# Squared-ReLU attention and two feed-forward networks on one core: another order where the last attention chunk meets the networks

## The chip, the cores and the metric

The kernel runs on one core of a Trainium2 chip. The metric is the device time of one execution in microseconds; the lower the better. Engines are named as in the profile: PE (matrix products; PEld loads their weights), DVE and ACT (element-wise work), POOL, and SP, which issues the transfers.

## The reference

```python
scores = (1.0 / S) * np.matmul(z, z.transpose(0, 2, 1))   # B=2, S=3008, d_qk=64
x = u * np.matmul(np.maximum(scores, 0.0) ** 2, v)        # d_model=256; then x: 6016 x 256
h = x @ w_in                                              # 256 -> 2048
y = (h - np.tanh(h)) @ w_out                              # 2048 -> 256
gate = 1.0 / (1.0 + np.exp(-(y @ w_gate)))                # 256 -> 1536
out = (gate * (y @ w_val)) @ w2_out                       # 1536 -> 256
```

The weights come as float64, everything else as float32.

## The kernel before, in words

The 6016 tokens are cut into 12 chunks of up to 512 (six to a batch; the last of each batch has 448). Every float32 operand of a product is split into a high and a low part, and a product is three passes: high by high, low weights by high, high weights by low.

The work is a list of **units** (`units`, L460 to L466). An attention unit is one chunk of queries against two tiles of 128 keys; there are 12 to a chunk (KP). The first 11 chunks are `HalfAttention`: its PE products use 64 rows of the array each, two at a time. The last chunk (11) is plain `Attention`, whose products use all 128 rows; its scores are four products over stacked high and low parts. A unit of the first network, `Ffn1`, takes 256 of the 2048 hidden columns (N1 = 8 units a chunk), one of the second, `Ffn2`, takes 128 of 1536 (N2 = 12). In this text A0 to A11 are the units of the last attention chunk, F*c*.*f* is unit f of `Ffn1` on chunk c, and G*c*.*f* one of `Ffn2`.

A unit has a `front` (its first PE products, into one of two PSUM buffers: `s`, `h` or `gv`), a `mid1` and `mid2` on ACT and DVE, and a `back` (PE products that add into `acc`). The loop at L562 takes a step per unit n: the small jobs noted in `todo` for n, the front of n, mid1 of n, mid2 of n-1, a pending `end`, and the backs of older units (`ahead`: two units on for attention, three for the networks). `end` runs one unit after the last back of a chunk; for `Ffn1` it copies `acc` into `yh` on ACT and writes `yl` on DVE, the two parts of y that every `Ffn2` front of the chunk reads. Each engine takes its instructions in the order in which this loop writes them.

The order of the units at the end of attention is set by sort keys (L462 to L466): A*i* has i; F0.f has START + f; F*c*.f for later chunks 12 + 12(c-1) + 1.5 f; G*c*.f has 12 + 12 c + f + LAG. Weights are split into high and low by `todo` jobs: two per `Ffn1` unit just ahead of it, and those of `Ffn2` from L535 on, W2_LAG units after F0.0.

Of the kernel before, what the change touches and what calls it, by code (L numbers as in the profile page):

```python
# [30 lines left out]
def squared_relu_attention__then__two_ffns(  # L31
# [24 lines left out]
    KP = KT // 2  # L56
# [3 lines left out]
    assert HALF * 2 == P and ND == 2 and DQ * 2 == P and KT % 4 == 0  # L60
    WARM, FILL = 6, 2
    LATE = 1
    START = 2.5
    LAG = 5
    W2_LAG = 16

    ring = ctx.enter_context(tc.tile_pool(name="ring", bufs=42))
    work = ctx.enter_context(tc.tile_pool(name="work", bufs=9))
# [19 lines left out]
    NC = len(chunks)  # L88
# [164 lines left out]
    class Attention(Unit):  # L253
# [5 lines left out]
            self.first, self.last = i == 0, i == KP - 1  # L259

        def front(self):
            b, n = self.b, self.n
            self.ps = psf.tile([P, 2, NQ], F32, tag="f", name="s")
            for e in range(2):
                i = 2 * self.i + e
                k = z_t[b, i // 4][:, 0, (i % 4) * P : (i % 4 + 1) * P]
                for h in range(2):
                    nc.tensor.matmul(self.ps[:, e, :n], k, z_t[b, self.j][:, h, :n], start=h == 0, stop=h == 1)  # L268
# [190 lines left out]
    N1, N2 = FF1 // P // 2, FF2 // P  # L459
    units = [HalfAttention(c, i) for c in range(NC - 1) for i in range(KP)]  # L460
    n_att = len(units)
    mixed = [(i, 0, Attention(NC - 1, i)) for i in range(KP)]  # L462
    mixed += [(START + f, 1, Ffn1(0, f)) for f in range(N1)]
    mixed += [(KP + (c - 1) * N2 + f * N2 / N1, 1, Ffn1(c, f)) for c in range(1, NC) for f in range(N1)]
    mixed += [(KP + c * N2 + f + LAG, 2, Ffn2(c, f)) for c in range(NC) for f in range(N2)]
    units += [t[2] for t in sorted(mixed, key=lambda t: t[:2])]  # L466
    start, where = {}, {}
    for n, u in enumerate(units):
# [6 lines left out]
    def at(n, fn):  # L475
        todo.setdefault(max(n, 0), []).append(fn)


    for b in range(B):
# [21 lines left out]
        for j in range(NZ):  # L501
            n = need[j] + early[j]
# [7 lines left out]
    for c in range(NC):  # L510
        at(start[0, c] + 2, lambda c=c: load_u(c))
        n = start[1, c]
# [7 lines left out]
    n = 8  # L520
    half = start[0, NZ]
    split = {}
    for k, p in enumerate(parts):
# [5 lines left out]
        if half - 14 < n < half + 4:  # L529
            n = half + 4  # L530
    for f in range(N1):
        n = where[1, 0, f]
        at(n - 3, split["wi1_", f // 2][f % 2])
        at(n - 2, split["wo1_", f // 2][f % 2])
    for f in range(N2 // 2):  # L535
        n = where[1, 0, 0] + W2_LAG + 2 * f
        assert n < where[2, 0, 2 * f]
        for i, key in enumerate(("wg2_", "wv2_", "wo2_")):
            at(min(n + i, where[2, 0, 2 * f] - (i < 2)), split[key, f // 2][f % 2])

    warm = const.tile([P, 1], F32, name="warm")
    square_max = const.tile([P, 1], F32, name="square_max")
# [86 lines left out]
```

## Time and profile before

| what | us |
|---|---|
| median of 3 executions (lowest, highest) | 1589.08 (1588.97, 1589.38) |
| the profiled execution | 1588.82 |
| its span, first to last instruction | 1587.0 |
| PE busy | 1578.1 |
| DVE busy | 1106.9 |
| ACT busy | 1039.8 |

The profile page shows for each engine how much of the span it is busy. A timeline row gives the start in us from the span's start, the time until the last of its instructions is done, the engine, line, operation, tile written and tiles read, shapes and count; in brackets stands idle time before it and who ended it. The time from one PE row's start to the next is what a row costs, since products overlap at their ends. The page's clock row stands at 9 (90% or more of full speed) in every slice, and the mean granted clock is 0.999.

### The profile page before, as it was taken

The numbers are of one execution on the slowest core, as the hardware profiler recorded it, in microseconds if no ns is written. First come the engines' busy times: TensorE is split into PE (matmuls) and PEld (weight loads), VectorE is DVE, ScalarE is ACT, GpSimd is POOL, SyncE is SP. The second block draws the span as 40 slices with busy tenths as digits, with TensorE's granted clock in tenths as the row PEclk, the third lists the DMA queues.
The fourth block names the chain that finished last, engine by engine and source line by source line (L and its number), as shares of the span: only waits on it lengthen the run. The fifth ranks groups of instructions, "written<-read, shape, count | busy, mean of one in ns | idle before, by whom it ended". The sixth has DMA issues, their size and how long they took to land.

```text
span 1587.0 us, 21490 instructions
## 1 busy us (share of the span) xinstructions
PE 1578.1 (99%) x8988; PEld 1339.8 (84%) x8988; DVE 1106.9 (70%) x1254; ACT 1039.8 (66%) x1249; POOL 0.2 (0%) x4
## 2 busy tenths in 40 slices
PE   9999999999999999999999999999999999999998
PEld 7888889888888788888888888888888888888888
DVE  8988898988788986566566656576656566655542
ACT  8667778666679976566665666666566665656532
POOL 0000000000000000000000000000000000000000
PEclk9999999999999999999999999999999999999999
DMA  6222232221100000000000000000000000000000
GB/s 226 81 81 80 86 114 79 81 81 54 39 27 1 23 3 0 27 1 15 12 1 25 1 27 1 27 0 1 25 0 27 0 27 1 0 26 1 14 1 25
DMA packets 28178, 53.28 MB, mean 34 GB/s; under 512 B 1969, under 2 KB 10161, under 8 KB 28081
## 3 DMA queue, kind: packets, MB, share of 16 engines
q1 hardware_dynamic: 28080, 51.91, 9.7%
q8 instruction: 70, 1.15, 0.3%
q14 instruction: 28, 0.22, 0.0%
HBM read 39.58 MB, written 12.32 MB: 33 GB/s over the span
## 4 chain that ended last, share of the span: by engine, by line
PE 96%; DVE 2%; issue 1%; ACT 1%; DMA 0%; DVEq 0%; SPq 0%
PE acc L234 30%; PE gv L246 24%; PE acc L346 20%; PE h L246 16%; PE s L313 5%; PE s L268 1%; DMA raw_wg<-w_gate 0%; DVE ah L329 0%; DVE e L80 0%; DVE z L80 0%; ACT a L327 0%; ACT a L324 0%; PE acc L559 0%; DVE th L393 0%; DVE al L80 0%
## 5 line engine op out<-in xcount | busy, mean ns | idle before, releaser
L80 DVE TENSOR_TENSOR e<-h,th 128x1024 f32<-128x1024 f32 (+1 forms) x96 | 115.4, 1202 | 285.0 <-ACT sq L388 285.0
L346 PE MATMUL acc<-ah,v 64*128 64x512 f32 (+1 forms) x2068 | 297.2, 385 | 0.7 <-DVE sum L360 0.7
L346 PEld LDWEIGHTS acc<-ah,v 64*128 64x128 f32 x2068 | 215.4, 184 | 30.9 <-DVE sum L360 1.3
L387 ACT ACTIVATE th<-h 128x1024 f32<-128x1024 f32 (+1 forms) x96 | 97.0, 1010 | 216.2 <-PE h L246 216.2
L246 PE MATMUL h<-xh,wi 128*128 128x512 f32 (+1 forms) x768 | 233.8, 386 | 0.8 <-DVE e L80 0.8
L234 PE MATMUL acc<-p,wo 128*128 128x512 f32 (+1 forms) x864 | 215.5, 385 | 0.0
L234 PE MATMUL acc<-gh,wo 128*128 128x512 f32 (+1 forms) x768 | 204.7, 386 | 0.5 <-DVE yl L80 0.4
L324 ACT ACTIVATE a<-s 128x1024 f32<-128x1024 f32 (+2 forms) x133 | 134.3, 1010 | 90.3 <-PE s L313 88.5
L234 PEld LDWEIGHTS acc<-p,wo 128*128 128x128 f32 x864 | 162.2, 188 | 30.0
L437 ACT ACTIVATE sg<-gv 128x512 f32<-128x512 f32 (+1 forms) x144 | 84.6, 588 | 156.7 <-PE gv L246 156.7
L346 PE MATMUL acc<-al,v 64*128 64x512 f32 (+1 forms) x1034 | 180.9, 386 | 0.1
L80 DVE TENSOR_TENSOR al<-a,ah 128x1024 fp32r<-128x1024 f32 (+3 forms) x146 | 173.6, 1189 | 7.6 <-DVE ah L329 0.5
L246 PE MATMUL gv<-yh,wg 128*128 128x512 f32 (+1 forms) x576 | 175.3, 385 | 0.0
L246 PE MATMUL gv<-yh,wv 128*128 128x512 f32 (+1 forms) x576 | 175.0, 385 | 0.0
L438 DVE TENSOR_TENSOR sg<-gv,sg 128x512 f32<-128x512 f32 (+1 forms) x144 | 98.3, 683 | 106.5 <-ACT sg L437 106.4
L246 PEld LDWEIGHTS h<-xh,wi 128*128 128x128 f32 x768 | 144.1, 188 | 28.3 <-DVE e L80 1.3
L234 PEld LDWEIGHTS acc<-gh,wo 128*128 128x128 f32 x768 | 144.1, 188 | 28.1 <-DVE yl L80 1.2
L246 PE MATMUL h<-xl,wi 128*128 128x512 f32 (+1 forms) x384 | 147.9, 385 | 0.0
L327 ACT ACTIVATE a<-a 128x1024 f32<-128x1024 f32 (+2 forms) x133 | 139.1, 1047 | 4.2
L393 DVE COPY_PREDICATED th<-m,e 128x1024 f32<-128x1024 uint32 (+1 forms) x96 | 131.7, 1371 | 10.2 <-ACT wv L194 0.5
L346 PEld LDWEIGHTS acc<-al,v 64*128 64x128 f32 x1034 | 111.3, 184 | 16.9 <-DVE al L80 2.8
L246 PEld LDWEIGHTS gv<-yh,wv 128*128 128x128 f32 x576 | 108.1, 188 | 20.2
(100 smaller groups left out, 2263.7 us busy)
## 6 DMA issues: line engine op xcount, KB each, us to landing
raw_wo<-w_out SPq DMA_DIRECT2D x14, 512.0 KB, 5.8
u<-uT SPq DMA_DIRECT2D x10, 512.0 KB, 7.3
x<-u SPq DMA_DIRECT2D x10, 512.0 KB, 3.1
xl<-x SPq DMA_DIRECT2D x10, 512.0 KB, 3.7
outT<-o SPq DMA_DIRECT2D x20, 256.0 KB, 2.1
vraw<-v SPq DMA_DIRECT2D x9, 512.0 KB, 6.5
raw_wi<-w_in SPq DMA_DIRECT2D x8, 512.0 KB, 8.6
zraw<-zT SPq DMA_DIRECT2D x12, 256.0 KB, 5.9
```

The lines of the kernel that those rows point to most:

```text
L80: nc.vector.tensor_tensor(out=out, in0=a, in1=b, op=ALU.subtract)
L234: nc.tensor.matmul(acc[d][:, :n], wt[:, wi, w, d * P : (d + 1) * P], hl[ai], start=first and m == 0, stop=last and m == len(passes) - 1,)
L246: nc.tensor.matmul(ps, w[:, wi, d, fi * P : (fi + 1) * P], xs[xi][:, d, :n], start=m == 0, stop=m == len(passes) - 1)
L268: nc.tensor.matmul(self.ps[:, e, :n], k, z_t[b, self.j][:, h, :n], start=h == 0, stop=h == 1)
L313: nc.tensor.matmul(self.ps[:, e, :n], z_t[b, i // 4][r, ki ^ x, c : c + P], q[r, qi ^ x, :n], start=m == 0, stop=m == 2)
L324: nc.scalar.activation(a[:, t, :n], self.ps[:, t, :n], AF.Relu, scale=SCALE)
L327: nc.scalar.activation(s, s, AF.Square)
L346: nc.tensor.matmul(acc[h][d][:, :n], vt[r, w, e, d * P : (d + 1) * P], self.hl[a][r, e, :n], start=self.first and banks[k] not in banks[:k ...
L387: nc.scalar.activation(t, h, AF.Tanh)
L393: nc.vector.copy_predicated(t, m.bitcast(U32), e)
L437: nc.scalar.activation(s[:, :n], self.ps[:, 0, :n], AF.Sigmoid)
L438: nc.vector.tensor_tensor(out=s[:, :n], in0=self.ps[:, 1, :n], in1=s[:, :n], op=ALU.mult)
```

## The change

Four edits.

- The first two units of the last attention chunk (A0, A1) make their scores with `HalfAttention.front`: six products of 64 rows in place of four of 128.
- START goes from 2.5 to 1.5: F0.0 comes after A1 and not after A2, and all of chunk 0's `Ffn1` a unit sooner.
- The units of G0 get keys 12 + 1 + f·16/12 in place of 12 + 5 + f: the first follows F1.0, and the twelve are spread over 16 key steps.
- The weights of `Ffn2` are split three units ahead of the G0 unit that first reads them; W2_LAG is gone.

```diff
-    START = 2.5
+    START = 1.5
     LAG = 5
-    W2_LAG = 16
+    LAG0 = 1
...
         def front(self):
+            if self.i < 2:
+
+                HalfAttention.front(self)
+                return
             b, n = self.b, self.n
...
-    mixed += [(KP + c * N2 + f + LAG, 2, Ffn2(c, f)) for c in range(NC) for f in range(N2)]
+    mixed += [(KP + LAG0 + f * (N2 + LAG - LAG0) / N2, 2, Ffn2(0, f)) for f in range(N2)]
+    mixed += [(KP + c * N2 + f + LAG, 2, Ffn2(c, f)) for c in range(1, NC) for f in range(N2)]
...
     for f in range(N2 // 2):
-        n = where[1, 0, 0] + W2_LAG + 2 * f
-        assert n < where[2, 0, 2 * f]
+        n = where[2, 0, 2 * f] - 3
         for i, key in enumerate(("wg2_", "wv2_", "wo2_")):
-            at(min(n + i, where[2, 0, 2 * f] - (i < 2)), split[key, f // 2][f % 2])
+            at(n + i, split[key, f // 2][f % 2])
```

What it does to the order shows best at three places. The names are those of the tiles; a number behind a name tells one buffer from another.

**DVE where y of chunk 0 is made.** `e`, `th`, `th` are the mid1 of an `Ffn1` unit, `gl` its mid2, `yl` the end of chunk 0. Before, the unit whose mid1 stands here is F1.1:

```order
L80 TENSOR_TENSOR e_6343<-h_6327,th_6341 128x1024
L392 TENSOR_TENSOR th_6341<-th_6341,sq_6340 128x1024
L393 COPY_PREDICATED th_6341<-m_6342,e_6343 128x1024
L80 TENSOR_TENSOR gl_6352<-th_6287,gh_6351 128x1024
L80 TENSOR_TENSOR yl0_6356<-acc0_5810,yh0_6355 128x512
L80 TENSOR_TENSOR yl0_6356<-acc1_5811,yh0_6355 128x512
```

Now it is F1.0, and behind `yl` stands at once `sg` of G0.0, which is made from y:

```order
L80 TENSOR_TENSOR e_6308<-h_6292,th_6306 128x1024
L396 TENSOR_TENSOR th_6306<-th_6306,sq_6305 128x1024
L397 COPY_PREDICATED th_6306<-m_6307,e_6308 128x1024
L80 TENSOR_TENSOR yl0_6317<-acc0_5790,yh0_6316 128x512
L80 TENSOR_TENSOR yl0_6317<-acc1_5791,yh0_6316 128x512
L442 TENSOR_TENSOR sg_6347<-gv_6334,sg_6347 128x512
```

On PE, between the front of F1.0 (`h_6292`) and the front of G0.0 (`gv_6334`) stands only the back of A10, 12 products, of which the last two and the next rows are:

```order
L234 MATMUL acc0_5699<-al_6244,v1_10_3459 128x448
L234 MATMUL acc1_5700<-al_6244,v1_10_3459 128x448
L246 MATMUL gv_6334<-yh0_6316,wg2_0_6232 128x512 x2
L246 MATMUL gv_6334<-yl0_6317,wg2_0_6232 128x512
L246 MATMUL gv_6334<-yh0_6316,wg2_0_6232 128x512 x2
```

The reader of y has moved up to one unit behind the end that writes it; before, three `Ffn1` fronts and backs lay between.

**DVE around the last unit of chunk 0's first network (F0.7).** Before, the split of chunk 1's x (`xl1`) stands ahead of F0.7's chain:

```order
L80 TENSOR_TENSOR xl1_6003<-xl1_6003,xh1_6185 128x1024
L80 TENSOR_TENSOR e_6204<-h_6188,th_6202 128x1024
L392 TENSOR_TENSOR th_6202<-th_6202,sq_6201 128x1024
L393 COPY_PREDICATED th_6202<-m_6203,e_6204 128x1024
L279 CAST ah_6220<-a_6217 128x2x448
```

Now it stands inside it, ahead of `gl`, which the back of F0.7 reads:

```order
L80 TENSOR_TENSOR e_6181<-h_6165,th_6179 128x1024
L396 TENSOR_TENSOR th_6179<-th_6179,sq_6178 128x1024
L397 COPY_PREDICATED th_6179<-m_6180,e_6181 128x1024
L80 TENSOR_TENSOR xl1_6026<-xl1_6026,xh1_6189 128x1024
L283 CAST ah_6200<-a_6197 128x2x448
L80 TENSOR_TENSOR al_6201<-a_6197,ah_6200 128x2x448
L80 TENSOR_TENSOR gl_6205<-th_6179,gh_6204 128x1024
```

ACT has the same move: `xh1` now stands between F0.7's four functions and A9's. On PE the back of F0.7 has come nearer too: after the front of F0.7 stand four score products of A9, the back of F0.6, the back of A8, eight score products (A10, A11), and then it. Before, the front of F1.0 lay between as well.

**DVE where y of chunk 1 is made.** Before, the two `yl` stand behind a unit of `Ffn2` and ahead of the next `Ffn1` chain:

```order
L438 TENSOR_TENSOR sg_6919<-gv_6906,sg_6919 128x512
L80 TENSOR_TENSOR p_6922<-sg_6887,p_6922 128x512
L80 TENSOR_TENSOR yl1_6926<-acc0_6439,yh1_6925 128x512
L80 TENSOR_TENSOR yl1_6926<-acc1_6440,yh1_6925 128x512
L80 TENSOR_TENSOR e_6953<-h_6937,th_6951 128x1024
```

Now they stand behind the chain of F2.1:

```order
L80 TENSOR_TENSOR e_6976<-h_6960,th_6974 128x1024
L396 TENSOR_TENSOR th_6974<-th_6974,sq_6973 128x1024
L397 COPY_PREDICATED th_6974<-m_6975,e_6976 128x1024
L80 TENSOR_TENSOR p_6984<-sg_6938,p_6984 128x512
L80 TENSOR_TENSOR yl1_6988<-acc0_6420,yh1_6987 128x512
L80 TENSOR_TENSOR yl1_6988<-acc1_6421,yh1_6987 128x512
```

The first back of chunk 2 (F2.0) writes into the PSUM buffers that these two read, so it waits for them. On PE, between the front of F2.1 and that back stand now the back of a G unit (6 products) and the front of another (12).

## Rows read from the trace of the kernel before

**Rows 1.** The page, part 1: PE busy, share of the span.

```profile
PE 1578.1 (99%) x8988; PEld 1339.8 (84%) x8988; DVE 1106.9 (70%) x1254; ACT 1039.8 (66%) x1249; POOL 0.2 (0%) x4
```

**Rows 2.** Waits of PE from 430 to 600 us: total, times, longest.

```profile
PE h L246 <- DVE e L80: 0.8, 1, 0.8
PE acc L234 <- DVE yl L80: 0.4, 1, 0.4
```

**Rows 3.** Stretches: length, busy time (instructions) of each engine, clock, DMA, GB/s.

```profile
444.65:448.61 3.96, 3.96 (x30) 2.84 (x28) 3.89 (x6) 3.36 (x5) 0.00 (x0) 1.00 0.00 0
...
541.02:543.74 2.72, 2.72 (x13) 2.06 (x11) 2.64 (x3) 2.72 (x5) 0.00 (x0) 1.00 0.00 0
543.74:547.50 3.76, 3.29 (x14) 2.36 (x14) 3.66 (x5) 3.70 (x5) 0.00 (x0) 1.00 0.00 0
...
552.94:556.80 3.86, 3.02 (x14) 2.37 (x14) 3.62 (x4) 3.72 (x5) 0.00 (x0) 1.00 0.71 240
556.80:559.84 3.04, 3.01 (x13) 2.17 (x12) 3.04 (x4) 3.00 (x5) 0.00 (x0) 1.00 0.00 0
```

**Rows 4.** Timeline of PE, where the pieces spoken of begin.

```profile
1.48 2.93 PE L559 MATMUL acc<-blank 128*128 128x512 f32 x6 [1.48 <-DVE blank L548]
...
449.63 0.73 PE L346 MATMUL acc<-ah,v 64*128 64x512 f32 x4
...
468.22 0.63 PE L234 MATMUL acc<-gl,wo 128*128 128x512 f32 x2
...
518.84 0.97 PE L268 MATMUL s<-z 128*128 128x448 f32 x4
...
528.38 1.07 PE L234 MATMUL acc<-gh,wo 128*128 128x512 f32 x4
...
536.27 0.97 PE L234 MATMUL acc<-ah,v 128*128 128x448 f32 x4
...
544.27 1.56 PE L234 MATMUL acc<-gh,wo 128*128 128x512 f32 x4 [0.38 <-DVE yl L80]
```

**Rows 5.** Timeline of DVE around F0.0.

```profile
458.49 1.22 DVE L364 TENSOR_TENSOR u<-sum,u 128x1024 f32<-128x1024 f32 x1
...
466.57 1.22 DVE L80 TENSOR_TENSOR gl<-th,gh 128x1024 fp32r<-128x1024 f32 x1
```

**Rows 6.** Timeline of ACT around F0.7.

```profile
517.40 1.04 ACT L220 CAST xh<-xl 128x1024 fp32r<-128x1024 f32 x1
519.04 1.03 ACT L387 ACTIVATE th<-h 128x1024 f32<-128x1024 f32 x1 [0.60 <-PE h L246]
...
523.17 0.90 ACT L274 ACTIVATE a<-s 128x896 f32<-128x896 f32 x1
...
525.17 1.05 ACT L400 CAST gh<-th 128x1024 fp32r<-128x1024 f32 x1
```

**Rows 7.** Timeline of DVE around F0.7.

```profile
519.24 1.22 DVE L80 TENSOR_TENSOR xl<-xl,xh 128x1024 fp32r<-128x1024 f32 x1
...
523.67 1.41 DVE L393 COPY_PREDICATED th<-m,e 128x1024 f32<-128x1024 uint32 x1
525.09 0.63 DVE L279 CAST ah<-a 128x896 fp32r<-128x896 f32 x1
...
526.83 1.22 DVE L80 TENSOR_TENSOR gl<-th,gh 128x1024 fp32r<-128x1024 f32 x1
```

**Rows 8.** Timeline of DVE where y of chunk 0 is made.

```profile
541.10 1.42 DVE L393 COPY_PREDICATED th<-m,e 128x1024 f32<-128x1024 uint32 x1
542.40 1.22 DVE L80 TENSOR_TENSOR gl<-th,gh 128x1024 fp32r<-128x1024 f32 x1
543.53 1.29 DVE L80 TENSOR_TENSOR yl<-acc,yh 128x512 fp32r<-128x512 f32 x2
```

**Rows 9.** Timeline of DVE where y of chunk 1 is made.

```profile
708.16 0.68 DVE L80 TENSOR_TENSOR p<-sg,p 128x512 fp32r<-128x512 f32 x1
708.76 1.28 DVE L80 TENSOR_TENSOR yl<-acc,yh 128x512 fp32r<-128x512 f32 x2
712.98 1.23 DVE L80 TENSOR_TENSOR e<-h,th 128x1024 f32<-128x1024 f32 x1 [2.94 <-ACT sq L388]
```

## The prediction

> **What bounds the kernel now.** I read the page first: PE is busy 99% of the span [rows 1], so only PE time counts, and a change pays only by fewer or cheaper products or by waits that PE no longer has. Then PE's own waits: between 430 and 600 us, where the change works, the list has two, 0.8 and 0.4 us [rows 2]. That list shows only time in which PE stands quite still. To see what a wait costs with all that follows, I cut PE's timeline into pieces of 12 full products. An undisturbed piece takes 2.72 us, so 0.227 a product; three pieces take 3.76, 3.86 and 3.04 [rows 3]. They lie where four fronts of the first network stand close together, F1.0 to F1.3, and ACT and DVE are full (3.7 of 3.8 us). The excess is 1.04 + 1.14 + 0.32 = 2.5 us. That is all that spreading G0 can win. Last I read the timelines of ACT and DVE around the four places where the change alters who stands ahead of whom, and asked there: when is the operand ready, and when does PE now come for it?
>
> **Scores of A0 and A1.** The stretch from A0's scores to A1's holds 4 score products and 24 products of 64 rows in pairs, and takes 3.96 us [rows 3]. In 64 rows the scores are three pairs of 448 columns, 3 × 0.227 × 448/512 = 0.60, and the 12 pairs behind them 12 × 0.227 = 2.72: 3.32 together, 0.64 less. A1's scores start at 448.61 and the next products at 449.63 [rows 4], 1.02 now, 0.60 then: 0.42 less. The change from 64 to 128 rows then comes once, at F0.0's front, as it came at A2's scores. The gain is 1.06, at least 0.4 (the products saved alone, 2 × 0.2) and at most 1.2.
>
> **G0 sooner and stretched.** `Ffn1` and `Ffn2` units now alternate, F1.0, G0.0, F1.1, G0.1 and so on; the three slow pieces go: -2.5 us, surely within -1.5 and -2.6.
>
> **Wait 1, F0.0's `gl`.** With START a unit lower, the product `u` of chunk 10 (`end`, L364) is written behind F0.0's mid1 and not ahead of it, so on DVE it stands between F0.0's predicated copy and its `gl`. `u` takes 1.13 us until the next can start (of its 1.22) [rows 5]. `gl` was done at 466.57 + 1.22 = 467.79, PE came for it at 468.22 [rows 4, 5]: 0.43 to spare. The pieces of PE between front and back of F0.0 are the same 40 products in another order. So 1.13 - 0.43 = **0.70** of new wait, between 0.3 and 0.9.
>
> **Wait 2, F0.7's back.** Let T be the end of F0.7's front, 518.84 [rows 4]. PE came to F0.7's back at 528.38, T + 9.54. Now there stand between 12 score products and 12 of A8's back, 448 columns each, and 12 of F0.6's back: 2 × 2.4 + 2.7 = 7.5 to 7.6. On ACT, A9's functions began at T + 4.33 and `gh` two us later [rows 6]; with `xh` in front (about 0.95) `gh` starts at T + 7.28 and is done at T + 8.33: 0.75 of wait. Then 4 products (0.91) to about T + 9.3. On DVE the predicated copy starts at T + 4.83 and holds DVE 1.30 us (to T + 6.13, as at 541.10 to 542.40 [rows 8]); `xl` adds 1.14, `ah` can begin at T + 7.27, and `gl` follows 1.74 behind `ah` (525.09 to 526.83 [rows 7]) and takes 1.22: done at T + 10.2. Another 0.95. Together **1.7**, between 1.0 and 2.0.
>
> **Wait 3, y of chunk 0.** In F1.1's step before, PE ended the front at 536.27 [rows 4]; DVE started the predicated copy 4.83 later, `gl` at 6.13, `yl` at 7.26, and the first `yl` was done 0.69 on; PE, which waited for it, went on at 544.27 [rows 4, 8], 8.0 after the front's end. So this row already shows the chain that now counts. Without `gl` in front the first `yl` is done 8.0 - 1.13 = 6.87 us after the front of F1.0. PE has until then only A10's back (2.4) and the two products of G0.0 that read `yh` (0.45): 6.87 - 2.85 = **4.0** us, nearly all of it PE standing still. ACT copies `yh` some 4.3 us after that front's end (519.04 - 0.20 to 523.17 for its four functions in F0.7 [rows 6]), so the first part of the wait (about 2.4) is put to `yh`, the second (about 1.5) to `yl`. Bounds 3.5 and 4.3.
>
> **Wait 4, y of chunk 1.** Because G0 is stretched, the end of F1 falls into the step of F2.1 and no longer into a step of `Ffn2`. Before, `yl` stood where DVE had nothing behind it for 2.94 us [rows 9]. Now it follows F2.1's chain and one `p` (0.60 from start to start [rows 9]): first `yl` at 6.13 + 0.60 + 0.69 = 7.4, the second at 8.0. PE comes to F2.0's back after 6 + 12 products, 4.08 us. Its first product waits 3.3, its second another 0.4: **3.7**, between 3.2 and 4.0.
>
> **Restarts.** The piece from 552.94 took 1.14 too long, with 0.84 of idle time in it [rows 2, 3]; about 0.2 to 0.3 goes when products start again. With four such places, partly in two halves, I add 0.6 (0 to 1.2).
>
> **What costs nothing.** The splits of the second network's weights (18 on ACT and on DVE, about 0.6 each) now come one to a unit. A pair of F and G units keeps PE 9.5 us; DVE has 5.1 of F's work, 1.2 of G's and 1.2 of splits, ACT less. Were that cover gone, a split would cost 0.6. SP's queue holds the same transfers in the same order; those of x come a unit sooner, and nothing waits for them now. From chunk 2 on the order is the old one.
>
> **Sum.** Gains 1.06 + 2.5 = 3.56. New waits 0.70 + 1.7 + 4.0 + 3.7 + 0.6 = 10.7. Net +7.1 on the profiled execution's 1588.82: 1595.9; the median of the runs lies 0.26 above that execution, so 1596.2. With every bound at its better end -3.8 + 8.0 = +4.2, at its worse end -1.9 + 12.4 = +10.5: 1593.3 to 1599.6. The waits add up because each is counted from the end of the front that starts its own chain, and a PE that came later from the wait before also starts that chain later.
>
> **Rivals.** *The clock falls in the long waits.* In the trace the longest stop inside the stretch is 0.84 us, and the granted clock stays 1.00 (2.4 GHz) behind it [rows 3]; so nothing here shows a stop of over 3 us. What slow products cost is seen at the start: the first six take 2.93 us [rows 4] where six take 1.36 at the later pace, 1.6 more. If one or both of waits 3 and 4 are followed by one or two such stretches, the time is 1.6 to 6 us more: 1598 to 1602. The Trainium skill, TensorE: Matmul & The Clock Gate, Part 1, says that an array left idle is put back to half clock; by it this is what wait 4, the longest in one piece, would bring. I give it 0.17, since wait 3 comes in two halves and wait 4 is short.
>
> *The hand-offs are covered.* Had DVE and ACT the copies of y ahead of the F unit's mid1, waits 3 and 4 would be gone, and -3.56 + 0.7 + 1.7 + 0.3 = -0.9: 1588.2; with the others covered as well 1585.5. It decides whether the first `yl` is ready within 2.9 us (G0.0) and 4.1 us (F2.0) of the front in whose step it stands. For it speaks chunk 1 before, where it cost PE nothing [rows 9]; against it the new order of DVE, with `yl` behind the predicated copy in both places, and 8.0 us measured [rows 4, 8]. 0.08. Half covered, for instance if one of waits 3 and 4 is only half as long: 1590 to 1593.3, 0.1.
>
> *The change doesn't do what it says.* The order of instructions shows all four edits, so this has no chance of its own.
>
> **How the numbers follow.** Forecast 1593.3 to 1599.6, chance 0.63, likeliest 1596.2; clock 0.17; half covered 0.1; covered 0.08; the rest unknown. Two in ten may be left out: the range is 1592.0 to 1600.5. About 0.2%, 3.2 us, is what a measurement of this kernel can tell from no change, so "same" is 1585.9 to 1592.3. Faster takes half of the covered case, 0.04; same the other half and a part of the half covered one, 0.1; slower 0.86.
>
> **What would show it.** Right: PE's waits list gets `gv` waiting on `yh` and `yl` (about 2.4 and 1.5 us), `acc` on `yl` (over 3 us, near 710 us, where y of chunk 1 is made), and two smaller ones on `gh` and `gl`; the waits on `e` and the old 0.4 on `yl` near 540 to 560 us are gone; A0's scores start 0.60 before the products behind them. Wrong: G0.0's front starts within 0.5 us of the end of A10's back, or F2.0's back does so behind the G front; then the hand-offs are covered. If products take 0.43 us behind a wait, or the granted clock falls under 1.00 there, the clock rival holds.

## The result, and the profile after

| what | before | after |
|---|---|---|
| median of 6 executions, us | 1589.06 | 1599.55 |
| lowest to highest | 1588.97 to 1589.38 | 1598.83 to 1600.06 |
| the profiled execution | 1588.82 | 1598.83 |
| its span | 1587.0 | 1597.1 |
| mean granted clock | 0.999 | 0.998 |

The change makes the kernel slower: ratio 1.0065, interval 1.0053 to 1.0077. That is 10.5 us on the medians and 10.0 on the two profiled executions, which the readings below compare. The prediction had 7.1 and a range up to 1600.5. The profiled execution of the changed kernel is the fastest of its six; the mean granted clock of the others is 0.996 to 0.998.

The page's busy times hardly differ from [rows 1], since what was lost is PE standing still or running slowly:

```profile
PE 1580.7 (99%) x8992; PEld 1355.5 (85%) x8992; DVE 1106.6 (69%) x1254; ACT 1040.0 (65%) x1249; POOL 0.2 (0%) x4
```

PE's waits of the changed kernel over the whole span (who waited, for whom; total, times, longest) answer to [rows 2]:

```profile
PE acc L234 <- DVE yl L80: 3.2, 1, 3.2
PE gv L246 <- ACT yh L420: 2.3, 1, 2.3
PE s L317 <- DVE z L80: 1.6, 2, 1.4
PE acc L563 <- DVE blank L552: 1.5, 1, 1.5
PE acc L234 <- DVE gl L80: 1.4, 2, 0.9
PE gv L246 <- DVE yl L80: 1.2, 1, 1.2
PE acc L350 <- DVE sum L364: 0.7, 1, 0.7
PE acc L234 <- ACT gh L404: 0.4, 1, 0.4
PE s L317 <- DVE z L109: 0.2, 1, 0.2
```

Three (`z`, `blank`, `sum`) are of the start and of attention and stand before too. The other five are the four announced waits, wait 3 in two halves, and the old waits on `e` and `yl` are gone. PE's timeline at the places of the change, in the columns of [rows 4]:

```profile
444.74 0.82 PE L317 MATMUL s<-z,z 64*128 64x448 f32 x6
445.34 1.14 PE L350 MATMUL acc<-ah,v 64*128 64x512 f32 x8
...
464.64 0.73 PE L234 MATMUL acc<-gl,wo 128*128 128x512 f32 x2 [0.54 <-DVE gl L80]
...
523.54 1.20 PE L234 MATMUL acc<-gh,wo 128*128 128x512 f32 x4 [0.37 <-ACT gh L404]
525.65 0.73 PE L234 MATMUL acc<-gl,wo 128*128 128x512 f32 x2 [0.90 <-DVE gl L80]
...
532.77 0.97 PE L234 MATMUL acc<-ah,v 128*128 128x448 f32 x4
...
537.70 0.73 PE L246 MATMUL gv<-yh,wg 128*128 128x512 f32 x2 [2.34 <-ACT yh L420]
539.60 0.50 PE L246 MATMUL gv<-yl,wg 128*128 128x512 f32 x1 [1.16 <-DVE yl L80]
...
543.42 1.14 PE L234 MATMUL acc<-ah,v 128*128 128x448 f32 x4
...
627.29 1.52 PE L234 MATMUL acc<-p,wo 128*128 128x512 f32 x6
...
634.69 1.74 PE L234 MATMUL acc<-gh,wo 128*128 128x512 f32 x4 [3.16 <-DVE yl L80]
...
639.51 0.63 PE L246 MATMUL h<-xh,wi 128*128 128x512 f32 x2
```

Two things are to be seen. A0's scores start at 444.74 and the products behind them 0.60 later, as announced. And behind waits 3 and 4 the products are slow: from 539.60 to 543.42 stand the ten products of G0.0 that were left, 3.82 us where ten take 2.27 at 0.227 each; from 634.69 to 639.51 stand the 12 of F2.0's back, 4.82 us where 12 take 2.72 (about 0.4 of it is a second stop, for the second `yl`). The granted clock (third figure from the end of a row, behind the five engines) says why; it falls to 0.50, the 1.2 GHz level, behind both waits:

```profile
540.00:541.00 1.00, 1.00 (x5) 0.78 (x4) 0.14 (x1) 0.00 (x0) 0.00 (x0) 0.68 0.00 0
541.00:542.00 1.00, 1.00 (x4) 0.81 (x3) 0.00 (x0) 0.00 (x0) 0.00 (x0) 0.50 0.07 16
...
636.00:637.00 1.00, 1.00 (x4) 0.80 (x3) 0.96 (x1) 0.00 (x0) 0.00 (x0) 0.50 0.00 0
...
639.00:640.00 1.00, 1.00 (x5) 0.77 (x5) 0.00 (x0) 0.00 (x0) 0.00 (x0) 0.83 0.00 0
```

PE is 1.00 busy in the slow microseconds, so these appear in no list of waits: the loss is in busy time. DVE's timeline at the two places of y answers to [rows 8, 9]; in both, `yl` stands right behind an `Ffn1` unit's predicated copy (chunk 1: and one `p`):

```profile
537.60 1.37 DVE L397 COPY_PREDICATED th<-m,e 128x1024 f32<-128x1024 uint32 x1
538.85 1.29 DVE L80 TENSOR_TENSOR yl<-acc,yh 128x512 fp32r<-128x512 f32 x2
...
632.12 1.35 DVE L397 COPY_PREDICATED th<-m,e 128x1024 f32<-128x1024 uint32 x1
633.35 0.69 DVE L80 TENSOR_TENSOR p<-sg,p 128x512 fp32r<-128x512 f32 x1
633.95 1.29 DVE L80 TENSOR_TENSOR yl<-acc,yh 128x512 fp32r<-128x512 f32 x2
```

Set against the same pieces of before, the profiled execution gives this sum:

| part | forecast, us | after's trace, us |
|---|---|---|
| A0 and A1 in 64 rows | -1.06 | -1.1 |
| G0 stretched | -2.5 | -2.5 (from 548.41 to 567.45 each 12 products take 2.72) |
| wait 1, F0.0 | 0.70 | 0.83 |
| wait 2, F0.7 | 1.7 | 1.88 |
| wait 3, standing still | 4.0 | 3.95 |
| wait 4, standing still | 3.7 | 3.7 |
| behind waits 3 and 4: slow clock and starting again | 0.6 for restarts, 0 for the clock | 1.74 + 1.7 |
| sum | +7.1 | +10.2 (measured +10.0) |

The last line but one comes from what the pieces last in all. From the end of A10's back (12 × 0.2025 behind 532.77, so 535.20) to the end of the G0.0 front 8.22 us pass where its 12 products take 2.72: 5.50, and 0.19 more in A11's back, still slow. 3.95 of the 5.69 are standing still with the start again behind it (537.70 - 535.20 = 2.50, and 539.60 - 537.70 less two products = 1.45), 1.74 are left for the slow clock and for starting again behind the second half of the stop. F2.0's back could have begun at 631.37 and ended at 634.09; it ended at 639.51, 5.42 later: 3.32 until its first product, about 0.4 between its first and second, 1.7 for the clock and for starting again. The run with filled stops below parts the two.

### The profile page after: what moved, and what is told of

It is laid out like the page before. It is cut to its first block, busy times and chain, and to the rows that moved or that the text cites. A ratio compares the mean times of both kernels' runs of the same rounds, so it can differ in the third digit from the quotient of the medians.

```text
span 1597.1 us, 21495 instructions
## 1 busy us (share of the span) xinstructions
PE 1580.7 (99%) x8992; PEld 1355.5 (85%) x8992; DVE 1106.6 (69%) x1254; ACT 1040.0 (65%) x1249; POOL 0.2 (0%) x4
## 4 chain that ended last, share of the span: by engine, by line
PE 95%; DVE 3%; ACT 1%; issue 1%; DMA 1%; DVEq 0%; SPq 0%
PE acc L234 29%; PE gv L246 24%; PE acc L350 20%; PE h L246 16%; PE s L317 5%; DMA raw_wg<-w_gate 0%; DVE th L396 0%; DVE e L80 0%; DVE al L80 0%; DVE ah L333 0%; ACT th L391 0%; DVE z L80 0%; PE s L272 0%; ACT sq L392 0%; DMA zraw<-zT 0%
## 5 line engine op out<-in xcount | busy, mean ns | idle before, releaser
L350 PEld LDWEIGHTS acc<-ah,v 64*128 64x128 f32 x2068 | 223.5, 184 | 23.2 <-DVE sum L364 1.5
L246 PEld LDWEIGHTS gv<-yh,wg 128*128 128x128 f32 x576 | 108.0, 188 | 22.8 <-ACT yh L420 2.7
L350 PEld LDWEIGHTS acc<-al,v 64*128 64x128 f32 x1034 | 115.6, 184 | 13.1 <-DVE al L80 2.7
```

The costliest lines, as they stand in the source:

```text
L246: nc.tensor.matmul(ps, w[:, wi, d, fi * P : (fi + 1) * P], xs[xi][:, d, :n], start=m == 0, stop=m == len(passes) - 1)
L350: nc.tensor.matmul(acc[h][d][:, :n], vt[r, w, e, d * P : (d + 1) * P], self.hl[a][r, e, :n], start=self.first and banks[k] not in banks[:k ...
```

## The experiments

Theory: the four waits and the clock behind two of them cost what the table says, waits 1, 3 and 4 because `end` stands behind mid1 in the queues of ACT and DVE. Rivals: the slow products behind waits 3 and 4 are the price of starting again after any stop, and not the clock's; and the G0 order costs by itself, because reader and writer stand near, whatever place `end` has. The first four kernels ran beside executions of before with a median of 1589.24, the last four beside 1589.69; so ratios compare better than microseconds.

**Only the scores in 64 rows** (before, with the first edit alone):

```
         def front(self):
+            if self.i < 2:
+
+                HalfAttention.front(self)
+                return
```

> The kernel before with only the first edit (scores of A0 and A1 in 64 rows). If four changes between 64 and 128 rows go and six products cost 0.60 us: 1.1 to 1.2 us less than before, 1587.9. If only the columns count (two times 0.2 us): 1588.7. No wait of PE is new.

Measured 1587.89 against 1589.24, ratio 0.9993 (0.9984 to 1.0002): 1.35 less, close to the term, though the interval takes in no change. PE's timeline shows the gain at its place, 1.13 us: from the start of A0's scores to the end of A2's pass 7.04 us (444.92 to 451.96) where before has 8.17 (444.65 to 452.82). A0's scores, and likewise A1's, take 0.61 until the next products start, where A1's took 1.02 before [rows 4]:

```profile
444.92 0.78 PE L317 MATMUL s<-z,z 64*128 64x448 f32 x6
445.53 1.10 PE L350 MATMUL acc<-ah,v 64*128 64x512 f32 x8
```

**G0 back in its old place** (after, with the old keys):

```
-    mixed += [(KP + LAG0 + f * (N2 + LAG - LAG0) / N2, 2, Ffn2(0, f)) for f in range(N2)]
-    mixed += [(KP + c * N2 + f + LAG, 2, Ffn2(c, f)) for c in range(1, NC) for f in range(N2)]
+    mixed += [(KP + c * N2 + f + LAG, 2, Ffn2(c, f)) for c in range(NC) for f in range(N2)]
```

> The changed kernel with the keys of G0 as before (12 + 5 + f); scores, START and weight splits stay changed. Theory (waits 3 and 4 and the slow clock behind them come from G0 being near and stretched): these 3.95 + 3.7 + 3.45 us go, the old slow pieces of F1.0 to F1.3 come back with 1.5 to 2.5 us: 1590 to 1591, and the granted clock is 1.00 all along. Rival (the loss hangs on START and the new scores): 1595 or more.

Measured 1589.03, ratio 0.9999 (0.9990 to 1.0008); clock 1.000. So the near and stretched G0, under this `end`, is what makes the difference of 10.5 us to after: waits 1 and 2 stay here, waits 3 and 4 and the slow clock are gone.

```profile
PE acc L234 <- DVE gl L80: 1.5, 2, 0.9
...
PE h L246 <- DVE e L80: 0.6, 1, 0.6
PE acc L234 <- ACT gh L404: 0.4, 1, 0.4
```

It came out 1 to 2 us better than expected. Of the three slow pieces of [rows 3] only about 1.2 us came back, at F1.4's front (554.23) and the backs on either side of it. F1.0's back takes 2.72 here and no longer waits for `yl`; that this is so because `Ffn1` comes a unit sooner is read from the order, not tested.

**Products that fill the stops** (after; ahead of the front of G0.0 ten and of G0.10 twelve products of zeros, into a buffer that the front then overwrites; nothing reads them):

```
+    FILLS = {(0, 0): 10, (0, 10): 12}
...
+            for _ in range(FILLS.get((self.c, self.f), 0)):
+                nc.tensor.matmul(self.ps[:, 1], blank[:, :P], blank, start=True, stop=True)
```

> The changed kernel with products of zeros that nothing reads: 10 ahead of the front of G0.0, 12 ahead of that of G0.10, 2.3 and 2.7 us, less than PE stands still there. Theory (3.45 us of the loss are products at half clock after stops of over 2 and 3 us): the stops get shorter, the clock stays at 1.00, and the time falls by 3 to 3.5 us to 1596.1. Rival (the products behind the waits are slow for another reason, or the clock falls with any wait): no change, 1599.5; if the zeros cost PE time they don't replace, up to 1604.

Measured 1595.72 (1595.61 to 1596.18), ratio 1.0042 (1.0028 to 1.0056): 3.8 us less than after, with 22 products more. The operands come no sooner: from the end of A10's back to G0.0's first product pass 2.51 us (2.50 in after), and `yl` still comes 1.17 later. Only the clock is now 1.00 behind the stops, and what follows is fast:

```profile
535.03 2.44 PE L436 MATMUL gv<-blank 128*128 128x512 f32 x10
537.54 0.73 PE L247 MATMUL gv<-yh,wg 128*128 128x512 f32 x2
539.45 0.50 PE L247 MATMUL gv<-yl,wg 128*128 128x512 f32 x1 [1.17 <-DVE yl L81]
...
632.92 1.55 PE L235 MATMUL acc<-gh,wo 128*128 128x512 f32 x4 [0.43 <-DVE yl L81]
```

```profile
541.00:542.00 1.00, 1.00 (x6) 0.84 (x5) 0.00 (x0) 0.00 (x0) 0.00 (x0) 1.00 0.00 0
```

That tells the two readings apart: PE still starts again behind a stop of 1.17 us and of 0.43, but the products after that are fast and the loss is gone. It also parts the table's last term. The ten products of G0.0 behind the stop take 2.40 us (3.82 in after, 2.27 undisturbed) and F2.0's back takes 3.23 (4.82 in after). So the clock cost 1.42 + 0.19 + 1.59 = 3.2 us, which is also the difference of the two profiled executions (1598.83 and 1595.62), and starting again costs 0.13 to 0.14 at each place. On the medians the two kernels are 3.8 apart, since the other executions of after are up to 1.2 us slower than the profiled one.

**`end` ahead of mid1** (after; the block that calls `end` goes ahead of `turn`, so the copies of y stand ahead of the `Ffn1` unit's functions on ACT and DVE):

```
+            if pending and n >= pending[0][0]:
+                _, u, a = pending.pop(0)
+                u.end(a)
             turn = any(u.last and isinstance(u, HalfAttention) for u in ready)
...
-            if pending and n >= pending[0][0]:
-                _, u, a = pending.pop(0)
-                u.end(a)
```

> The changed kernel with the pending end of a chunk written ahead of the step's mid1, so that yh, yl (and u) stand ahead of the next unit's functions on ACT and DVE; PE's order is the same. Theory (waits 1, 3 and 4 are the place of the end in the queues of ACT and DVE): they and the slow clock go, wait 2 stays with 1.9: 1589.1 - 3.7 + 1.9 = 1587.3, at most 1588. Rival (G0 simply stands too near for PE, whatever the other engines' order): waits of 2 us and more stay on yh and yl, 1593 or more.

Measured 1588.14, ratio 0.9994 (0.9985 to 1.0002): 11.4 us less than after, with every unit where the change put it. DVE writes `yl` before F1.0's mid1 even begins (its `e` comes 3.3 us later), and PE goes from A10's back to G0.0 without a stop; in the list of its waits neither `yh` nor `yl` is left:

```profile
532.02 1.28 DVE L80 TENSOR_TENSOR yl<-acc,yh 128x512 fp32r<-128x512 f32 x2
535.35 1.23 DVE L80 TENSOR_TENSOR e<-h,th 128x1024 f32<-128x1024 f32 x1 [2.04 <-ACT sq L392]
```

```profile
535.20 0.57 PE L234 MATMUL acc<-al,v 128*128 128x448 f32 x2
535.61 0.62 PE L246 MATMUL gv<-yh,wg 128*128 128x512 f32 x2
```

```profile
PE acc L234 <- DVE gl L80: 1.1, 2, 0.9
...
PE acc L234 <- ACT gh L404: 0.4, 1, 0.4
```

So nearness alone costs nothing here; the place of `end` in two queues does. The time is some 0.8 us over what was expected. Wait 2 is whole (1.88), but that stood in the expected sum. What did not stand there: about half of wait 1 is left (F0.0's back takes 3.26, 0.54 too long, with 0.22 of standing still for `gl`), since `u`, now ahead of F0.0's `e` on DVE, holds that up until 457.58. And the profiled execution reaches A0's scores at 445.51, where after does at 444.74, so 0.8 us went before any unit that the change moved. The other three kernels with `end` ahead of mid1 reach them at 445.4 to 445.9, the kernels without at 444.6 to 445.1; `end` runs for the attention chunks too, but that its place is what costs this is not shown.

**The same move in the kernel before** (no other edit):

> The kernel before with only the end of a chunk written ahead of the step's mid1. Theory (the end waits in the queues behind mid1): the piece of 3.76 us at the back of F1.0, which waited for yl, falls to about 2.72, the other two slow pieces stay: 1.0 us less, 1588.1. Rival (the order of ACT and DVE there doesn't matter, or the copies of y delay F1.1): 1589.1 or more.

Measured 1588.78, ratio 0.9994 (0.9985 to 1.0003), 0.9 us less; the wait on `yl` is gone and that on `e` is down to 0.24. In its trace F1.0's back takes 2.72 again, as expected, though the interval takes in no change. In before `end`'s place was worth about 1 us; the change made it worth 11.

**Chunk 1's split of x a unit earlier** (on top of `end` ahead of mid1), to test wait 2:

```
-        at(n - 3, lambda c=c: split_x(c))
+        at(n - 3 - (c == 1), lambda c=c: split_x(c))
```

> The changed kernel with the end ahead of mid1 and the split of chunk 1's x a unit sooner, so that xh and xl stand ahead of F0.7's functions as before. Theory (1.2 us of wait 2 are xh and xl, the rest is that F1.0's front no longer lies between): the excess at F0.7's back falls from 1.9 to 0.7 us, the time from 1588.1 to 1587.0. Rival (wait 2 comes from PE's order alone): 1588.1.

Measured 1587.32, ratio 0.9986 (0.9976 to 0.9995). At F0.7's back the wait on `gh` is gone and that on `gl` is 0.55 instead of 0.93; in all the piece is 0.87 us over its undisturbed length, in place of 1.88. So `xh` and `xl` ahead of `gh` and `gl` made a good half of wait 2. That the rest is PE coming sooner was not run by itself; in the next run, where the split stands as early as in before and F1.0's front lies again between F0.7's front and back, the wait is gone whole.

```profile
524.96 0.73 PE L234 MATMUL acc<-gl,wo 128*128 128x512 f32 x2 [0.55 <-DVE gl L80]
```

**Chunk 0 a unit later** (START 2.5 and LAG0 2, with `end` ahead of mid1):

```
-    START = 1.5
+    START = 2.5
...
-    LAG0 = 1
+    LAG0 = 2
```

> The changed kernel with the end ahead of mid1, START back at 2.5 and the first G0 unit a key step later (behind F1.1). Theory: no wait of the four is left, and the gains stand alone: 1589.15 - 1.3 - 2.5 = 1585.4, at most 1586. Rival (G0 near and stretched can't be had without a wait): over 1587.

Measured 1586.10, ratio 0.9978 (0.9969 to 0.9987), 3.6 us under before. All waits of PE in this kernel are those of the start and of attention:

```profile
PE acc L563 <- DVE blank L552: 1.5, 1, 1.5
PE s L317 <- DVE z L80: 1.4, 1, 1.4
PE acc L350 <- DVE sum L364: 0.7, 1, 0.7
```

That is the sum of the two gains without any of the waits: the forecast had 3.56 for them, here 3.6 (2.1 to 4.9 by the interval). The trace agrees from A0's scores on: 1138.70 us to the end of the span (445.50 to 1584.2), where before takes 1142.35 (444.65 to 1587.0). No piece between 538 and 568 us is slow: 12 products take 2.71 to 2.73. It is faster than before and after.

**The same, with `end` behind mid1 again:**

> As the run before, but with the end behind mid1 as in the changed kernel. Only wait 3 is left, now in F1.1's step with gl ahead of yl: 7.95 us from the end of F1.1's front to the first yl, less 2.03 for A11's back and 0.45 for two products: 5.5 us, and about 1.7 for the clock behind it. Theory: 1589.15 - 3.8 + 7.2 = 1592.6. Without loss by the clock: 1590.9. Rival (START one unit sooner was what made the waits): 1586.

Measured 1593.46, ratio 1.0024 (1.0015 to 1.0034), 7.4 us above the run before it, for the place of `end` alone. Waits 1, 2 and 4 aren't there; wait 3 is now one stop of 3.7 us and a second of 0.9, and the clock falls while PE still stands:

```profile
541.46 1.22 PE L246 MATMUL gv<-yh,wg 128*128 128x512 f32 x2 [3.69 <-ACT yh L420]
543.55 0.79 PE L246 MATMUL gv<-yl,wg 128*128 128x512 f32 x1 [0.86 <-DVE yl L80]
...
547.48 0.40 PE L246 MATMUL gv<-yl,wv 128*128 128x512 f32 x1
```

```profile
540.00:541.00 1.00, 0.00 (x0) 0.00 (x0) 0.90 (x2) 1.00 (x2) 0.00 (x0) 0.77 0.00 0
541.00:542.00 1.00, 0.54 (x1) 0.50 (x2) 1.00 (x2) 0.98 (x3) 0.00 (x0) 0.50 0.00 0
```

All 12 products of G0.0 run slow: from 541.46 to 547.71 are 6.25 us, less 0.86 of standing still and 2.72 for 12 products, 2.7 us for the clock and for starting again. The expected time had 1.7 there; the measured one is 0.9 over it.

## Why the prediction was right or wrong

**Sign and range: right.** Slower had a chance of 0.86; the time lies inside the range, 3.4 us above the predicted one. That it does is partly luck: the range had its upper end from larger waits, the waits came at their forecast sizes, and what filled the space was a loss that the sum did not hold.

**The gains: right.** The scores alone gave 1.35 on the medians, over the bound of 1.2, but 1.13 in the trace (1.06 forecast); both gains together gave 3.6 where all waits were gone (3.56 forecast).

**The waits: right in place and size.** The chain counted for wait 3, first `yl` done 6.87 us after the end of F1.0's front, put PE's next product at 532.77 + 6.87 = 539.64; it began at 539.60. For wait 4 the same counting, 7.4 us after F2.1's front (627.29), gave 634.69, and that is where it began. Waits 1 and 2 are 0.83 and 1.88 with the start behind the stop, which takes 0.13 at each; without it they are 0.70 and 1.74, for 0.70 and 1.7 forecast. "What costs nothing" held as well: PE waits for no split of weights in any of these traces.

**The step that failed is the price of what follows a long stop.** The sum had 0.6 for "Restarts" and nothing for the clock, judged from a stop of 0.84 us behind which the clock stayed at 1.00. The restarts were right: 0.13 to 0.14 at each of the four places, 0.5 in all. The clock was not nothing: behind waits 3 and 4 it fell to 0.50 and cost 3.2 us. With that the sum is +10.3, against +10.0 measured. So the rival that was given 0.17 came in, on top of the forecast and at both places: 1598 to 1602 had been written for it, 1599.55 was measured. Its price, 1.6 us for a stretch of slow products taken from the start [rows 4], was right as well (1.61 and 1.59); only its chance was wrong. The reasons against it were that wait 3 comes in two halves and that wait 4 is short. Neither counted: two products between stops of 2.34 and 1.16 us did not hold the clock, nor did a stop of 3.16 leave it alone. The sentence from the Trainium skill, TensorE: Matmul & The Clock Gate, Part 1, that an idle array is put back to half clock, agrees with the trace at both places (0.50), though the clock fell there only when PE was at work again.

**Two smaller slips.** Wait 4 was looked for near 710 us; it is at 634.69. The cause is that [rows 9] are not of chunk 1's y but of chunk 2's. Chunk 1's stand 92 us earlier in the trace of before, and since the order repeats there, they read alike (0.60 from `p` to `yl`, 2.94 idle behind), so the sum did not suffer:

```profile
615.68 0.68 DVE L80 TENSOR_TENSOR p<-sg,p 128x512 fp32r<-128x512 f32 x1
616.28 1.28 DVE L80 TENSOR_TENSOR yl<-acc,yh 128x512 fp32r<-128x512 f32 x2
620.50 1.23 DVE L80 TENSOR_TENSOR e<-h,th 128x1024 f32<-128x1024 f32 x1 [2.94 <-ACT sq L388]
```

**The rival "the hand-offs are covered"** did not come in, but what it asked for, the copies of y ahead of mid1, is what `end` ahead of mid1 does. Its price was 1588.2, and 1588.14 was measured; that they meet so closely is luck in part, since half of wait 1 went too and 0.8 us was lost elsewhere.

**What stays open.** The gain of the stretched G0 was not run by itself. Its 2.5 is read from traces: where before has its three slow pieces, 12 products take 2.72 in after and in the run with chunk 0 a unit later, against 2.5 us more in before. Its two moves were not run apart either: that the near start makes wait 3 and the stretching wait 4 is read from the order of instructions and the waits. Why only about 1.2 us of the slow pieces came back with the old G0 order was read from the waits, not tested.

## What to carry to other kernels

When a reader is moved close behind its writer, count what stands ahead of the writer in the queue of its own engine: here four functions on ACT and three on DVE that had nothing to do with y made 7.7 us of waiting, and three lines moved in the loop took it away. The gain itself (3.6 us) showed only when the two smaller waits were gone as well. A stop of PE as long as those here (3.16 and 3.69 us, or 2.34 and 1.16 with two products between) is not paid at its own length: look at the granted clock behind it, and add the slow products to its price. A stop that can't be removed can still be filled: 22 products that nothing reads made this kernel 3.8 us faster.

## What the runs showed of the hardware

- Two full products between a stop of 2.34 and one of 1.16 us did not keep the clock up; it fell to 0.50 somewhat under a microsecond after work had begun again at 539.60, with PE 1.00 busy (0.68 in the microsecond from 540), so the first products behind the stop are not the slow ones.
- In the last run, with a stop of 3.7 us, it fell while PE stood (0.77 in the microsecond from 540, in which PE was not busy at all) and the loss, starting again included, was 2.7 us instead of 1.7.
- Products of zeros count like others: with ten in the first stop and 1.17 us of standing still behind them, and twelve ahead of the other with 0.43, the clock stayed at 1.00.
